# Attention with chunk selection and a gated FFN: 32-row score tiles for batch 0, plain v loads, later weight scaling, two jobs moved to ScalarE, finer preparation

## The chip, the cores and the metric

The kernel runs on one core of a Trainium2 chip. The metric is the device time of one execution in microseconds, the median of several runs. A run is called slow when it is over 1.5% above the fastest of its kernel; slow runs are left out of every comparison. The profile is one execution taken with the hardware profiler.

## The reference, cut to what matters

Four batches, eight heads, 768 positions, head size 64. Keys are grouped in 24 chunks of 32. For every query a bound on its score with each chunk is computed, the six best causal chunks are kept, and ordinary softmax attention runs over these. All heads of a token, side by side, then go through RMS normalisation and a gated FFN.

```python
ub = np.sum(np.maximum(q[:, :, :, None, :] * k_min[:, :, None, :, :],
                       q[:, :, :, None, :] * k_max[:, :, None, :, :]), axis=-1)
ub = np.where(causal, ub, -1000000000.0)
top_chunks = np.argsort(ub, axis=-1)[..., -top_k:]
scores = scale * np.matmul(q, k.transpose(0, 1, 3, 2))
scores = np.where(mask, scores, -1000000000.0)      # mask: chosen chunks, causal
# ... softmax, times v, heads side by side: x of 3072 x 512 ...
xn = x / np.sqrt(np.mean(x * x, axis=-1, keepdims=True) + 1e-06) * rms_g
g = xn @ w_gate
val = xn @ w_val
return (g * (1.0 / (1.0 + np.exp(-g))) * val) @ w_out
```

## The kernel before: the parts that matter

A *quad* is four heads of one batch, so there are eight quads, two per batch. The preparation of a quad loads K and Q, transposes them on VectorE in 32-row blocks (kT, qT), finds chunk minima and maxima, computes the bounds on TensorE (ubp), and ranks and chooses chunks on VectorE (mk, mt). The score matmuls want one head's 64 rows of K or Q plus 24 mask rows on partitions 0 to 87. The transposes leave two halves of 32 rows for four heads instead, so DMAs move them:

```python
def to_bf16(nm, dst, eng):
    def go():
        hb = half.tile([P, 2, S], BF16, name="hb")
        eng.tensor_copy(hb[:], st[nm + "T"][:])           # GpSimd
        for dh in range(2):
            for a in range(4):
                nc.sync.dma_start(out=dst[bi][32 * dh:32 * (dh + 1), a, :],
                                  in_=hb[32 * a:32 * (a + 1), dh, :])
    return go
# choose(): four more moves bring the chosen-chunk mask to QH[D:KR]
# scores(): per head and key block, one matmul of 88 rows
nc.tensor.matmul(sc[:, hl, 256 * e:256 * e + qn],
                 KH[bi][0:KR, a, kb * P:(kb + 1) * P], QH[bi][0:KR, a, qs:qs + qn],
                 start=True, stop=True)
```

v is loaded by casting DMAs from GpSimd's queue, ahead of the three FFN weights, which are casting DMAs too. The weights are multiplied by rms_g in place on VectorE (`fold_g`), directly after quad 0's preparation in the program. The tail of attention for one block of 128 tokens is:

```python
def rms(tt):
    nc.vector.tensor_tensor_reduce(out=junk[:], in0=xnat[tt][:], in1=xnat[tt][:],
        scale=1.0 / DM, scalar=0.0, op0=ALU.mult, op1=ALU.add, accum_out=ss_all[:, tt:tt + 1])
    # GpSimd: ri = (ss + eps) ** -0.5
    nc.vector.tensor_scalar(out=xs[:], in0=xnat[tt][:], scalar1=ri, scalar2=None, op0=ALU.mult)
    return xs
# turn(): TensorE transposes xs; after 512 tokens the FFN pieces gp, vp, ... op are queued
```

The emitted program is reordered: a scheduler places each instruction in its engine's queue by data dependencies and estimated times. The order on an engine is therefore not simply that of the text. In the traces below nothing passes an instruction that waits: while VectorE stood 13.25 us for wg, the choice of quad 0 stood behind it.

The softmax here doesn't subtract the row's maximum and nothing guards it: scores larger than these inputs give would overflow.

## Time and profile before

| | before |
|---|---|
| time, median of the runs beside the changed kernel's | 438.75 us |
| profiled span | 433.3 us |
| TensorE busy / VectorE / ScalarE / GpSimd | 320.6 / 258.9 / 178.7 / 183.4 us |
| first score matmul, first FFN matmul (gp) | 62.0 us, 107.4 us |

The first fence is the busy share of the span in 40 slices of 10.8 us, as tenths, of TensorE and of the core's DMA engines.

```profile
PE   0230084099897994888769986889899998789996
DMA  9999936170199254821562517102100020002002
```

In the first five slices the DMA engines are nearly full and TensorE nearly idle. The second fence is the table of engine time by stretch. Its columns are stretch, length, busy time with instruction counts for TensorE, its weight loads, VectorE, ScalarE and GpSimd, then clock, DMA share and GB/s. The cuts are the first score and the first gp.

```profile
0.00:62.00 62.00, 12.34 (x30) 7.66 (x30) 34.02 (x70) 1.28 (x1) 24.72 (x46) 0.75 1.14 162
62.00:107.40 45.40, 26.68 (x210) 19.00 (x211) 31.48 (x66) 19.47 (x24) 11.62 (x18) 0.62 0.45 101
107.40:433.30 325.90, 281.57 (x1905) 154.30 (x1903) 193.43 (x408) 157.90 (x240) 147.06 (x165) 0.94 0.30 60
```

For 107 us TensorE does 39 us of work. After that it is busy 281.6 of 325.9 us, idle 44.3. The timeline (start, duration, engine, line, instruction; in brackets the idle time before it and what ended it) shows what the start waits for:

```profile
32.99 2.21 DVE L392 TENSOR_SCALAR wg<-wg,rmsg 128x1536 bf16<-128x1536 bf16 x4 [13.25 <-DMA wg<-in_moe_w_gate_dram]
40.35 2.21 DVE L392 TENSOR_SCALAR wv<-wv,rmsg 128x1536 bf16<-128x1536 bf16 x4 [5.15 <-DMA wv<-in_moe_w_val_dram]
57.31 5.00 SPq L160 DMA_DIRECT2D QH_127<-hb  x8
62.04 0.33 PE L269 MATMUL sc<-QH_127,KH_124 88*128 88x256 bf16 x2 [0.52 <-DMA QH_127<-hb]
86.54 1.59 PE L269 MATMUL sc<-QH_128,KH_125 88*128 88x256 bf16 x6 [12.79 <-DMA QH_128<-hb]
```

VectorE stands 18.4 us for the weights, with quad 0's choice and quad 1's whole preparation behind it in its queue. The moves of a quad's Q then stand before its first scores. Later, TensorE's largest wait (engine, line, what it waited for: us in total, number, longest) and three groups of VectorE instructions (count, then busy us and mean ns of one, then idle time before) are these:

```profile
PE tp L342 <- DVE xs L331: 21.4, 12, 3.2
```

```profile
L323 DVE CUSTOM_DVE_ANT_0 junk<-xnat 128x512 bf16<-128x512 bf16 x24 | 22.6, 941 | 0.6
L280 DVE TENSOR_TENSOR pt<-pt,tri 128x1024 bf16<-128x1024 bf16 x24 | 19.1, 796 | 15.1 <-ACT pt L275 15.0
L380 DVE COPY osb<-op 128x512 f32<-128x512 f32 x24 | 16.6, 690 | 39.6 <-PE op L375 36.8 <-PE avn L298 2.8
```

### The profile page before, as it was taken

To read this page: it belongs to the slowest core of one execution; us is meant where nothing else is said; L and a number is where in the kernel's file an instruction comes from. 1 tells how busy PE (TensorE), PEld (TensorE's weight loads), DVE (VectorE), ACT (ScalarE), POOL (GpSimd) and SP (SyncE) were. 2 spreads that over 40 slices of the span, in tenths; PEclk is the share of its full clock that TensorE was granted. 3 is DMA by queue.
4 is the path that set the end of the run, shared out by engine and by line. 5 is a ranking of instruction groups with operands and counts; after the bars stand their busy time and mean duration, and the time that the engine had idled before them with its cause. 6 is when DMAs were issued, how large, how long until landed. Compare 5 with 4: busy or idle time off the path is not lost.

```text
span 433.3 us, 6106 instructions
## 1 busy us (share of the span) xinstructions
PE 320.6 (74%) x2144; PEld 181.0 (42%) x2144; DVE 258.9 (60%) x544; ACT 178.7 (41%) x265; POOL 183.4 (42%) x229
## 2 busy tenths in 40 slices
PE   0230084099897994888769986889899998789996
PEld 0120043067354463553435643554555554334442
DVE  5804947558858459759933798365746346623331
ACT  1000013075576322745831355532684456531750
POOL 9720210332597414563652168522443224530650
PEclk9985575558999896799959998799999999989999
DMA  9999936170199254821562517102100020002002
GB/s 163 181 210 210 109 101 137 48 173 20 31 145 120 51 166 78 97 73 28 130 59 84 147 40 73 39 0 78 67 2 8 29 75 1 2 0 98 0 2 97
DMA packets 52318, 34.32 MB, mean 79 GB/s; under 512 B 29504, under 2 KB 48192, under 8 KB 52288
## 3 DMA queue, kind: packets, MB, share of 16 engines
q1 hardware_dynamic: 24592, 26.07, 24.2%
q0 software_dynamic: 27696, 7.87, 19.2%
q8 instruction: 17, 0.28, 0.3%
q14 instruction: 13, 0.11, 0.1%
HBM read 28.31 MB, written 6.29 MB: 80 GB/s over the span
## 4 chain that ended last, share of the span: by engine, by line
PE 39%; DVE 27%; DMA 11%; issue 9%; POOL 8%; ACT 3%; SPq 3%; POOLq 0%; DVEq 0%; ACTq 0%
PE op L375 12%; PE gp L357 8%; PE vp L357 8%; DMA wv<-in_moe_w_val_dram 6%; DVE qT L148 4%; PE sc L269 4%; DVE tg L366 4%; PE ubp L209 4%; DVE xs L331 3%; PE avn L298 3%; DVE junk L323 3%; POOL ri_all L329 2%; DMA vext<-in_v_dram 2%; DVE kT L148 2%; DVE xnat L312 2%
## 5 line engine op out<-in xcount | busy, mean ns | idle before, releaser
L275 ACT ACTIVATE pt<-sc 128x768 bf16<-128x768 f32 (+1 forms) x96 | 84.3, 916 | 142.3 <-PE sc L269 140.6
L370 POOL TENSOR_TENSOR hh<-tg,vs 128x512 bf16<-128x512 bf16 x72 | 84.3, 1174 | 93.2 <-ACT vs L364 37.9
L357 PE MATMUL gp<-xsT,wg 128*128 128x512 bf16 x288 | 78.2, 392 | 3.7 <-DVE tg L366 2.1
L357 PE MATMUL vp<-xsT,wv 128*128 128x512 bf16 x288 | 76.7, 388 | 1.0 <-DVE tg L366 0.6
L366 DVE SCALAR_TENSOR_TENSOR tg<-th,gp 128x512 bf16<-128x512 bf16 x72 | 49.0, 681 | 46.3 <-ACT th L362 46.2
L375 PE MATMUL op<-wo,hh 128*128 128x512 bf16 x288 | 65.8, 383 | 0.0
L362 ACT ACTIVATE th<-gp 128x512 bf16<-128x512 f32 x72 | 43.3, 602 | 53.7 <-PE gp L357 53.6
L364 ACT ACTIVATE vs<-vp 128x512 bf16<-128x512 f32 x72 | 43.2, 600 | 21.4 <-PE vp L357 17.8
L298 PE MATMUL avn<-vext,pt 128*128 128x65 bf16 x672 | 38.6, 206 | 12.9 <-DVE xnat L312 6.2
L298 PEld LDWEIGHTS <-pt 128*128 128x128 bf16 x672 | 33.4, 106 | 28.9 <-DVE xnat L312 10.5
L357 PEld LDWEIGHTS <-wv 128*128 128x128 bf16 x288 | 28.8, 100 | 37.1 <-issue 6.0
L375 PEld LDWEIGHTS <-hh 128*128 128x128 bf16 x288 | 27.9, 99 | 31.9 <-issue 1.1
L380 DVE COPY osb<-op 128x512 f32<-128x512 f32 x24 | 16.6, 690 | 39.6 <-PE op L375 36.8
L357 PEld LDWEIGHTS <-wg 128*128 128x128 bf16 x288 | 27.1, 100 | 28.7 <-issue 7.5
L269 PE MATMUL sc<-QH_128,KH_125 88*128 88x256 bf16 (+1 forms) x144 | 22.4, 282 | 15.2 <-DMA QH_128<-hb 13.0
L209 PE MATMUL ubp<-qT,BD_131 128*128 128x288 f32 x32 | 11.1, 469 | 29.9 <-DVE qT L148 29.9
L269 PE MATMUL sc<-QH_127,KH_124 88*128 88x256 bf16 (+1 forms) x144 | 25.9, 319 | 3.8 <-DMA QH_127<-mt 2.5
L133 POOL DMA_DIRECT2D vext<-in_v_dram x32 | 27.5, 864 | 1.5 <-DMA vext<-in_v_dram 1.5
L280 DVE TENSOR_TENSOR pt<-pt,tri 128x1024 bf16<-128x1024 bf16 x24 | 19.1, 796 | 15.1 <-ACT pt L275 15.0
L342 PE MATMUL tp<-ident,xs 128*128 128x128 bf16 x96 | 11.4, 253 | 21.7 <-DVE xs L331 21.7
L148 DVE STREAM_TRANSPOSE qT<-qraw 128x768 f32<-128x768 f32 x16 | 23.8, 1532 | 4.6 <-POOL hb L157 4.0
L148 DVE STREAM_TRANSPOSE kT<-kraw 128x768 f32<-128x768 f32 x16 | 24.0, 1534 | 3.7 <-DMA kraw<-in_k_dram 3.7
(79 smaller groups left out, 347.6 us busy)
## 6 DMA issues: line engine op xcount, KB each, us to landing
kraw<-in_k_dram SPq DMA_DIRECT2D x32, 192.0 KB
qraw<-in_q_dram SPq DMA_DIRECT2D x32, 192.0 KB
out_dram<-osb SPq DMA_DIRECT2D x24, 256.0 KB
vext<-in_v_dram POOLq DMA_DIRECT2D x32, 96.0 KB, 6.0
wg<-in_moe_w_gate_dram POOLq DMA_DIRECT2D x1, 1536.0 KB, 21.2
wv<-in_moe_w_val_dram POOLq DMA_DIRECT2D x1, 1536.0 KB, 27.4
wo<-in_moe_w_out_dram POOLq DMA_DIRECT2D x1, 1536.0 KB, 32.0
KH_124<-hb SPq DMA_DIRECT2D x24, 48.0 KB
```

The costliest lines, as they stand in the source:

```text
L133: nc.gpsimd.dma_start(out=vext[:, :, a, 0:D], in_=v[b, 4 * g + a, :, :].rearrange("(blk pp) d -> pp blk d", pp=P),)
L148: nc.vector.transpose(out=st[nm + "T"][:, dh, :].rearrange("p (m r j) -> p m j r", r=32, j=4), in_=st[nm + "raw"][:, :, :, dh, :],)
L209: nc.tensor.matmul(ubp[:, 0:W], bd[:, t, :], rhs, start=(t == 0), stop=(t == 3))
L269: nc.tensor.matmul(sc[:, hl, 256 * e:256 * e + qn], KH[bi][0:KR, a, kb * P:(kb + 1) * P], QH[bi][0:KR, a, qs:qs + qn], start=True, stop=True,)
L275: nc.scalar.activation(out=pt[:, 2 * hp:2 * hp + 2, 0:W], in_=sc[:, :, 0:W], func=ACT.Exp, scale=SCALE,)
L298: nc.tensor.matmul(avn[:, a, :], pts[kg][:, a, off:off + P], vext[:, kb, a, :], start=(kb == 0 and a == 0), stop=(kb == nkb - 1 and a == 3 ...
L357: nc.tensor.matmul(ps[:], w[:, g, ht * P:(ht + 1) * P], x[:, g, :], start=(g == 0), stop=(g == NP - 1),)
L362: nc.scalar.activation(out=th[:], in_=gp[:], func=ACT.Tanh, scale=0.5)
L364: nc.scalar.activation(out=vs[:], in_=vp[:], func=ACT.Copy, scale=0.5)
L366: nc.vector.scalar_tensor_tensor(out=tg[:], in0=th[:], scalar=1.0, in1=gp[:], op0=ALU.add, op1=ALU.mult,)
L370: nc.gpsimd.tensor_tensor(out=hh[ht][:], in0=tg[:], in1=vs[:], op=ALU.mult)
L375: nc.tensor.matmul(op[:], hh[ht][:, t * P:(t + 1) * P], wo[:, ht, :], start=(ht == 0), stop=(ht == NHT - 1),)
```

## The change

The intent is to start attention earlier and to keep TensorE supplied. Batch 0 (quads 0 and 1) scores straight from the transposed layout on 32-row tiles, with the mask as a third 32-row product, so that no operand is moved. v comes by plain loads from SyncE's queue and is cast on GpSimd. The scaling by rms_g is emitted later. Square sums and output copies go to ScalarE. Preparation, score halves and rms transposes are spread over a unit. Cut to its core:

```diff
-    raw = ctx.enter_context(tc.tile_pool(name="raw", bufs=2))
+    raw = ctx.enter_context(tc.tile_pool(name="raw", bufs=5))        # now shared by k, q and v
-            nc.gpsimd.dma_start(
-                out=vext[:, :, a, 0:D],
+            nc.sync.dma_start(
+                out=t[:, :, a, :],
                 in_=v[...].rearrange("(blk pp) d -> pp blk d", pp=P),
+        def v_bf16():
+            nc.gpsimd.tensor_copy(VX[bi][:, :, :, 0:D], st["vraw"][:])
+                if tiled:                                            # to_bf16, quads 0 and 1
+                    nc.scalar.activation(out=dst[bi][:, 0:2, :], in_=st[nm + "T"][:], func=ACT.Copy)
+                    return
+            if tiled:                                                # choose
+                nc.vector.transpose(out=QH[bi][:, 2, Q0:S], in_=mk[:].rearrange("p j c -> p (j c)"))
+                return
+    def scores_tiled(u):                                             # per key block
+            for t in range(3):                                       # two halves of K.Q, then the mask
+                for a in range(4):                                   # head a on rows 32a to 32a+31
+                    r = slice(32 * a, 32 * (a + 1))
+                    o = sc[a // 2][:, a % 2, :]                      # a PSUM bank per head
+                    ...
-        if last:                                                     # causal product, four heads
+        if last:                                                     # now once per two heads
-        nc.vector.tensor_tensor_reduce(out=junk[:], ...)
+        nc.scalar.activation(out=junk[:], in_=xnat[tt][:], func=ACT.Square, ...)
-            nc.vector.tensor_copy(osb[:], op[:])
+            nc.scalar.activation(out=osb[:], in_=op[:], func=ACT.Copy)
-    fold_g()                                                         # after quad 0's preparation
+        if i >= 5 and folds:                                         # at the end of units 5 and 6
+            folds.pop(0)()
-            scores(units[i + 1])
+            scores(units[i + 1], 0)
         fill(1)
-        for f in late:
-            f()
+        prep_step(rate // 2)
+            scores(units[i + 1], 1)
         ...
         fill(1)
+        prep_step(rate - rate // 2)
+        while late and late[0][0] <= i:                              # the rms transposes
+            late.pop(0)[1]()
```

Not shown: the mask rows of a K buffer are now rewritten in every quad from 2 on, four small copies and a memset on VectorE. There are also fewer buffers for the exp tiles (4 instead of 5) and for the FFN's tiles (2 instead of 3).

More of the change, by code (lines that the diff above doesn't have):

```diff
@@ L55 @@
     persist = ctx.enter_context(tc.tile_pool(name="persist", bufs=1))
-    raw = ctx.enter_context(tc.tile_pool(name="raw", bufs=2))
+    raw = ctx.enter_context(tc.tile_pool(name="raw", bufs=5))
     tpose = ctx.enter_context(tc.tile_pool(name="tpose", bufs=1))
     half = ctx.enter_context(tc.tile_pool(name="half", bufs=1))
-    vpool = ctx.enter_context(tc.tile_pool(name="vpool", bufs=3))
     sel = ctx.enter_context(tc.tile_pool(name="sel", bufs=2))
-    ptp = ctx.enter_context(tc.tile_pool(name="ptp", bufs=5))
+    ptp = ctx.enter_context(tc.tile_pool(name="ptp", bufs=4))
     xnp = ctx.enter_context(tc.tile_pool(name="xnp", bufs=8))
@@ L65 @@
     hhp = ctx.enter_context(tc.tile_pool(name="hhp", bufs=NHT + 4))
-    ffn = ctx.enter_context(tc.tile_pool(name="ffn", bufs=3))
+    ffn = ctx.enter_context(tc.tile_pool(name="ffn", bufs=2))
     psS = ctx.enter_context(tc.tile_pool(name="psS", bufs=2, space=bass.MemoryType.PSUM))
@@ L84 @@
         nc.gpsimd.memset(own[32 * a:32 * (a + 1), a, :], 1.0)
+    chunkrow = const.tile([P, S], BF16, name="chunkrow")
+    nc.gpsimd.memset(chunkrow[0:32, :], MASKED)
+    nc.gpsimd.affine_select(
+        out=chunkrow[0:32, :], in_=chunkrow[0:32, :], compare_op=ALU.is_ge, fill=0.0,
+        base=0, pattern=[[1, S]], channel_multiplier=-CH,
+    )
+    nc.gpsimd.affine_select(
+        out=chunkrow[0:32, :], in_=chunkrow[0:32, :], compare_op=ALU.is_ge, fill=0.0,
+        base=CH - 1, pattern=[[-1, S]], channel_multiplier=CH,
+    )
+    for a in range(1, 4):
+        nc.vector.tensor_copy(chunkrow[32 * a:32 * (a + 1), :], chunkrow[0:32, :])
     eps6 = const.tile([P, 1], FP32, name="eps6")
@@ L93 @@
     NKB = 3
+    NTILED = NG
+    VX = [persist.tile([P, NT, 4, D + 1], BF16, name=f"VX{i}") for i in range(NKB)]
     KH = [persist.tile([P, 4, S], BF16, name=f"KH{i}") for i in range(NKB)]
@@ L122, in load @@
         for nm, src in (("k", k), ("q", q)):
-            t = raw.tile([P, NT, 4, 2, CH], FP32, name=nm + "raw")
+            t = raw.tile([P, NT, 4, 2, CH], FP32, name=nm + "raw", tag="raw")
             for a in range(4):
@@ L129, in load, with load_v @@
             st[nm + "raw"] = t
-        vext = vpool.tile([P, NT, 4, D + 1], BF16, name="vext")
-        nc.gpsimd.memset(vext[:, :, :, D:D + 1], 1.0)
+    def load_v(qd):
+        st = quads[qd]
+        t = raw.tile([P, NT, 4, D], FP32, name="vraw", tag="raw")
         for a in range(4):
-            nc.gpsimd.dma_start(
-                out=vext[:, :, a, 0:D],
-                in_=v[b, 4 * g + a, :, :].rearrange("(blk pp) d -> pp blk d", pp=P),
+            nc.sync.dma_start(
+                out=t[:, :, a, :],
+                in_=v[st["b"], 4 * st["g"] + a, :, :].rearrange("(blk pp) d -> pp blk d", pp=P),
             )
-        st["vext"] = vext
+        st["vraw"] = t
     def prep_pieces(qd):
@@ L152, in transpose_half, with chunk_rows @@
             return go
+        tiled = qd < NTILED
+        def v_bf16():
+            nc.gpsimd.tensor_copy(VX[bi][:, :, :, 0:D], st["vraw"][:])
+        def chunk_rows():
+            for a in range(4):
+                nc.vector.tensor_copy(KH[bi][D:KR, a, :], chunkrow[D:KR, :])
+            nc.vector.memset(QH[bi][D:KR, :, 0:Q0], 0.0)
         def to_bf16(nm, dst, eng):
             def go():
+                if tiled:
+                    nc.scalar.activation(out=dst[bi][:, 0:2, :], in_=st[nm + "T"][:], func=ACT.Copy)
+                    return
                 hb = half.tile([P, 2, S], BF16, name="hb")
@@ L241, in choose @@
                 )
-        return [
+        return ([] if tiled else [chunk_rows]) + [
             transpose_half("k", 0), transpose_half("k", 1),
@@ L248, in prep_pieces, with score_spans, scores @@
             to_bf16("q", QH, nc.gpsimd),
-            upper(0), upper(1), rank(0), rank(1), choose,
+            upper(0), upper(1), rank(0), rank(1), choose, v_bf16,
         ]
     xnat = {}
-    def scores(u):
+    def score_spans(u):
+        qd, qt, kg = u["key"]
+        last = kg == qt
+        for e in range(2):
+            qs = qt * 256 + (128 if (last and e) else 0)
+            yield e, 2 * kg + e, qs, (qt + 1) * 256 - qs
+    def scores_tiled(u):
+        qd, qt, kg = u["key"]
+        kb_, qb_ = KH[qd % NKB], QH[qd % NKB]
+        sc = [psS.tile([P, 2, 512], FP32, name="sc", tag="sc") for _ in range(2)]
+        for e, kb, qs, qn in score_spans(u):
+            ks = slice(kb * P, (kb + 1) * P)
+            ms = max(qs, Q0)
+            for t in range(3):
+                for a in range(4):
+                    r = slice(32 * a, 32 * (a + 1))
+                    o = sc[a // 2][:, a % 2, :]
+                    if t < 2:
+                        nc.tensor.matmul(
+                            o[:, 256 * e:256 * e + qn], kb_[r, t, ks], qb_[r, t, qs:qs + qn],
+                            start=(t == 0), stop=False, skip_group_check=True,
+                        )
+                    else:
+                        nc.tensor.matmul(
+                            o[:, 256 * e + ms - qs:256 * e + qn], chunkrow[r, ks],
+                            qb_[r, 2, ms:qs + qn],
+                            start=False, stop=True, skip_group_check=True,
+                        )
+        return sc
+    def scores(u, hp):
         qd, qt, kg = u["key"]
@@ L259, in scores @@
         W = 384 if last else 512
-        pt = ptp.tile([P, 4, 512], BF16, name="pt")
-        for hp in range(2):
+        if hp == 0:
+            u["pt"] = ptp.tile([P, 4, 512], BF16, name="pt")
+            if qd < NTILED:
+                u["sc"] = scores_tiled(u)
+        pt = u["pt"]
+        if qd < NTILED:
+            sc = u["sc"][hp]
+        else:
             sc = psS.tile([P, 2, 512], FP32, name="sc", tag="sc")
@@ L264, in scores @@
                 a = 2 * hp + hl
-                for e in range(2):
-                    kb = 2 * kg + e
-                    qs = qt * 256 + (128 if (last and e) else 0)
-                    qn = (qt + 1) * 256 - qs
+                for e, kb, qs, qn in score_spans(u):
                     nc.tensor.matmul(
@@ L274, in scores @@
                     )
-            nc.scalar.activation(
-                out=pt[:, 2 * hp:2 * hp + 2, 0:W], in_=sc[:, :, 0:W], func=ACT.Exp, scale=SCALE,
-            )
+        hs = slice(2 * hp, 2 * hp + 2)
+        nc.scalar.activation(out=pt[:, hs, 0:W], in_=sc[:, :, 0:W], func=ACT.Exp, scale=SCALE)
         if last:
-            dg = pt[:].rearrange("p a (e w) -> p a e w", e=2)[:, :, :, 0:P]
+            dg = pt[:, hs, :].rearrange("p a (e w) -> p a e w", e=2)[:, :, :, 0:P]
             nc.vector.tensor_tensor(
                 out=dg, in0=dg,
-                in1=tri[:].unsqueeze(1).unsqueeze(1).to_broadcast([P, 4, 2, P]),
+                in1=tri[:].unsqueeze(1).unsqueeze(1).to_broadcast([P, 2, 2, P]),
                 op=ALU.mult,
             )
-        u["pt"] = pt
     def values(u, s, avn, kgs, pts):
         qd, qt, _ = u["key"]
-        vext = quads[qd]["vext"]
+        vext = VX[qd % NKB]
         nkb = 2 * qt + s + 1
@@ L321, in rms @@
     def rms(tt):
-        junk = ev.tile([P, DM], BF16, name="junk")
-        nc.vector.tensor_tensor_reduce(
-            out=junk[:], in0=xnat[tt][:], in1=xnat[tt][:], scale=1.0 / DM,
-            scalar=0.0, op0=ALU.mult, op1=ALU.add, accum_out=ss_all[:, tt:tt + 1],
+        junk = ev.tile([P, DM], BF16, name="junk", bufs=1)
+        nc.scalar.activation(
+            out=junk[:], in_=xnat[tt][:], func=ACT.Square, scale=DM ** -0.5,
+            accum_out=ss_all[:, tt:tt + 1],
         )
@@ L387, in queue_ffn, with fold_g @@
             ffn_queue.append(lambda t=t: project(t))
-    def fold_g():
-        for w in (wg, wv):
-            for g in range(NP):
-                nc.vector.tensor_scalar(
-                    out=w[:, g, :], in0=w[:, g, :], scalar1=rmsg[:, g:g + 1],
-                    scalar2=None, op0=ALU.mult,
-                )
+    def fold_g(w):
+        for g in range(NP):
+            nc.vector.tensor_scalar(
+                out=w[:, g, :], in0=w[:, g, :], scalar1=rmsg[:, g:g + 1],
+                scalar2=None, op0=ALU.mult,
+            )
     load(0)
-    nc.sync.dma_start(out=rmsg[:], in_=moe_rms_g.rearrange("(g p) -> p g", p=P))
+    load(1)
     nc.vector.memset(BD[0][:], 0.0)
     nc.vector.memset(BD[1][:], 0.0)
-    nc.gpsimd.memset(KH[0][D:KR, 0, :], MASKED)
-    nc.gpsimd.affine_select(
-        out=KH[0][D:KR, 0, :], in_=KH[0][D:KR, 0, :], compare_op=ALU.is_ge, fill=0.0,
-        base=0, pattern=[[1, S]], channel_multiplier=-CH,
-    )
-    nc.gpsimd.affine_select(
-        out=KH[0][D:KR, 0, :], in_=KH[0][D:KR, 0, :], compare_op=ALU.is_ge, fill=0.0,
-        base=CH - 1, pattern=[[-1, S]], channel_multiplier=CH,
-    )
-    for i in range(NKB):
-        nc.vector.memset(QH[i][D:KR, :, 0:Q0], 0.0)
-        for a in range(4):
-            if i or a:
-                nc.vector.tensor_copy(KH[i][D:KR, a, :], KH[0][D:KR, 0, :])
-    load(1)
+    for i in range(NKB):
+        nc.vector.memset(VX[i][:, :, :, D:D + 1], 1.0)
+    for piece in prep_pieces(0)[:-1]:
+        piece()
+    load_v(0)
+    nc.sync.dma_start(out=rmsg[:], in_=moe_rms_g.rearrange("(g p) -> p g", p=P))
     nc.gpsimd.dma_start(out=wg[:], in_=moe_w_gate.rearrange("(kt p) n -> p kt n", p=P))
@@ L419 @@
     nc.gpsimd.dma_start(out=wo[:], in_=moe_w_out.rearrange("(kt p) n -> p kt n", p=P))
-    for piece in prep_pieces(0):
-        piece()
-    fold_g()
+    load_v(1)
+    prep_pieces(0)[-1]()
     NQD = B * NG
@@ L441 @@
     pts: dict = {}
-    scores(units[0])
+    scores(units[0], 0)
+    scores(units[0], 1)
+    folds = [lambda: fold_g(wg), lambda: fold_g(wv)]
     for i, u in enumerate(units):
@@ L450 @@
                 load(loaded)
+                load_v(loaded)
         if i + 1 < len(units):
             nxt = units[i + 1]["key"][0]
-            if nxt >= prep_next - 1:
-                if nxt == prep_next - 1:
-                    prep_step(len(prep_queue))
-            scores(units[i + 1])
+            if nxt == prep_next - 1:
+                prep_step(len(prep_queue))
+        ahead = first_of.get(prep_next - 1, i) - 2 - i
+        rate = -(-len(prep_queue) // max(1, ahead))
+        if i + 1 < len(units):
+            scores(units[i + 1], 0)
         fill(1)
-        for f in late:
-            f()
-        late = []
+        prep_step(rate // 2)
+        if i + 1 < len(units):
+            scores(units[i + 1], 1)
         if kg == 0:
@@ L466 @@
         values(u, 0, avn, [kg], pts)
-        rate = -(-len(prep_queue) // max(1, first_of.get(qd + 1, i + 1) - 1 - i)) if prep_queue else 0
-        rate = max(rate, 3)
-        prep_step(rate)
+        done = []
+        if kg == qt:
+            done.append(normalise(u, 0, avn))
         fill(1)
+        prep_step(rate - rate // 2)
+        while late and late[0][0] <= i:
+            late.pop(0)[1]()
         if kg == qt:
-            done = [normalise(u, 0, avn)]
             avn = psV.tile([P, 4, D + 1], FP32, name="avn", tag="av")
@@ L478 @@
                     xs = rms(tt)
-                    late.append(lambda tt=tt, xs=xs: turn(tt, xs))
-    for f in late:
+                    late.append((i + 1, lambda tt=tt, xs=xs: turn(tt, xs)))
+        if i >= 5 and folds:
+            folds.pop(0)()
+    for _, f in late:
+        fill(1)
         f()
```

## The prediction

> **What bounds the kernel now** (timeline and table of engine time by stretch; profiled span 433.3 us, timed median 437.6, so some 4 us lie outside the span).
>
> 1. Until the first FFN matmul (gp) at 107.4 us TensorE is mostly empty: 12.3 us busy in 0:62, 26.3 us in 62:107. The bound is a chain through VectorE and DMA. VectorE meets the folding of rms_g early in its in-order queue and stands 13.25 us for wg and 5.15 us for wv, until 40.3 us, with DMA over 90% busy. Only at 42.5 us does it go on to quad 0's selection and quad 1's preparation. The first score runs at 62.0 us, after eight QH moves. TensorE then waits 12.8 us, until 86.5, for quad 1's QH moves.
> 2. From 107 us on TensorE is the bound, with holes: idle about 44 of 326 us by the stretches. The largest wait is transposes for xs (21.4 us, 12 waits), the end of the chain square sum, GpSimd rsqrt, xs.
>
> **What the change does, costed.**
> - Folding moves behind both selections of batch 0: 18.4 us of waiting leave the start. On the path, all of it.
> - Batch 0 takes K, Q and mask straight from the transposes. Its 32 K/Q moves and 8 mask moves go; four ScalarE casts come (estimate 1.3 us each, from exp: 0.81 us for 768 columns, 0.97 for 1024). A unit has 24 score matmuls instead of 8 (which took 0.82 us). The Trainium skill ("TensorEngine Tiling (Array Packing)", Key Properties) says that row tiles run in parallel and that a mode switch drains the array. The four heads write four PSUM banks, so I expect 0.7 to 1.2 us a unit: neutral. No trace shows it yet.
> - v: 27.5 us of GpSimd issue go, eight casts of about 1.5 us come; off the path.
> - 24 square sums and 24 output copies (0.69 us each, 33 us) leave VectorE; about 29 us (0.6 each) come to ScalarE, 41% busy before. VectorE gains some 8 us of mask rows. The rms transposes come half a step later, preparation in smaller pieces. This should close 10 to 20 us of the holes; I take 16.
>
> **Sum.** In the instruction order that the changed kernel builds to: quad 0 selected near 28 us, first exp near 29, quad 1 selected near 48, first gp near 72 (estimate: 23 us of VectorE work lie between that selection and the first tg), 35 us earlier. Some 7 us more TensorE work is then left. Span 433 - 35 + 7 - 16 = 389, with the 4 us outside 393 us. Range 376 to 410. Chances: faster by over 2% 0.97, within 2% 0.02, slower 0.01.
>
> **What would show each step.**
> - No 13 and 5 us of VectorE idle before folding; folding near 45 to 57 us.
> - First score before 32 us, first gp at 65 to 80 us, no 12.8 us hole.
> - Transposes' wait on xs under 12 us; TensorE idle after the first gp 25 to 35 us.
> - Four row-tiled matmuls starting within about one matmul's time.
> - Busy: VectorE about 235 us, ScalarE 212, GpSimd 165.
>
> **What would make it wrong.** Row tiles running one after the other (estimate 2.5 us a unit, up to 20 us). q, k, v landing late behind weights that now start earlier. ScalarE holding exp behind a square sum. The five shared raw buffers holding loads back. The gain could shrink to 25 us; if the holes close fully it could reach 65.

## The result

| | before | after |
|---|---|---|
| time, median | 438.75 us | 394.05 us (393.0 to 396.0, four runs) |
| profiled span | 433.3 us | 391.3 us |
| TensorE / VectorE / ScalarE / GpSimd busy | 320.6 / 258.9 / 178.7 / 183.4 | 319.8 / 238.9 / 211.2 / 158.0 us |
| first score, first gp | 62.0, 107.4 us | 24.3, 71.8 us |

The ratio is 0.897, with a 95% interval of 0.890 to 0.905. Ratios here are the mean time of one kernel's fast runs over the mean of the other's fast runs of the same rounds, so not quite the ratio of the medians. The same views of the kernel after follow, slices first (9.8 us each):

```profile
PE   0165687998799649967798899798999999799996
DMA  8999999100068159111960196023110110002002
```

From the third slice on TensorE is busy for half a slice or more, while the loads still run. The table by stretch, cut at the first scores that need quad 0's choice and at the first gp:

```profile
0.00:27.40 27.40, 6.66 (x25) 4.22 (x26) 20.39 (x47) 4.25 (x3) 9.89 (x25) 1.00 1.02 213
27.40:71.80 44.40, 31.05 (x334) 19.88 (x334) 33.23 (x74) 21.71 (x31) 11.46 (x18) 0.59 1.05 198
71.80:391.30 319.50, 282.11 (x1981) 156.27 (x1978) 185.29 (x399) 185.28 (x308) 136.60 (x150) 0.95 0.28 66
```

The start is 35.6 us shorter (107.4 less 71.8), the rest 6.4 us (325.9 less 319.5). TensorE's work in the rest is the same (282.1 against 281.6 us). Its idle time there fell from 44.3 to 37.4 us. In the timeline the weights are folded without a wait, and no move stands before a score:

```profile
24.29 0.40 PE L306 MATMUL sc<-QH_134,KH_131 32*128 32x256 bf16 x8
27.40 0.21 PE L311 MATMUL sc<-QH_134,chunkrow 32*128 32x64 bf16 x4 [2.71 <-DVE QH_134 L266]
47.43 1.28 DVE L455 TENSOR_SCALAR wg<-wg,rmsg 128x1536 bf16<-128x1536 bf16 x1
71.84 1.75 PE L421 MATMUL gp<-xsT,wg 128*128 128x512 bf16 x4
```

TensorE's waits after the first gp, the counterpart of the wait on xs. The transposes' wait on xs is gone from the list of that window, and smaller waits have taken its place:

```profile
PE avn L362 <- DVE pt L345: 5.0, 7, 1.6
PE sc L335 <- DMA QH_134<-hb: 5.0, 2, 4.8
PE vp L421 <- DVE tg L430: 4.0, 4, 2.3
PE tp L406 <- DVE tg L430: 3.5, 5, 1.4
PE gp L421 <- DVE tg L430: 3.5, 4, 1.4
PE vp L421 <- ACT vs L428: 3.1, 4, 2.2
```

Of the three VectorE groups two have left for ScalarE. The third, the causal product, is cut in halves and costs more than before:

```profile
L387 ACT ACTIVATE junk<-xnat 128x512 bf16<-128x512 bf16 x24 | 15.2, 631 | 12.5 <-DVE xnat L376 12.5
L345 DVE TENSOR_TENSOR pt<-pt,tri 128x512 bf16<-128x512 bf16 x48 | 30.3, 637 | 21.1 <-ACT pt L342 20.7
L444 ACT ACTIVATE osb<-op 128x512 f32<-128x512 f32 x24 | 14.2, 600 | 34.4 <-PE op L439 31.1 <-issue 3.2
```

One thing the prediction had not seen in any trace can now be read: the cost of row tiles at full clock. This is a whole unit between values and gp. From its first start to the start of gp its 24 matmuls take 0.76 us (86.53 to 87.29). The last two lines are from the kernel before: a full unit of 8 matmuls of 88 rows took 0.88 us by the same measure (132.44 to 133.32).

```profile
86.53 0.40 PE L306 MATMUL sc<-QH_135,KH_132 32*128 32x256 bf16 x8
86.76 0.28 PE L311 MATMUL sc<-QH_135,chunkrow 32*128 32x256 bf16 x4
86.86 0.39 PE L306 MATMUL sc<-QH_135,KH_132 32*128 32x256 bf16 x8
87.08 0.28 PE L311 MATMUL sc<-QH_135,chunkrow 32*128 32x256 bf16 x4
87.29 0.39 PE L421 MATMUL gp<-xsT,wg 128*128 128x512 bf16 x1
132.44 1.04 PE L269 MATMUL sc<-QH_129,KH_126 88*128 88x256 bf16 x8
133.32 0.60 PE L357 MATMUL gp<-xsT,wg 128*128 128x512 bf16 x2
```

The prediction's 0.82 us for 8 matmuls is another thing: the units of before with that figure lie on the diagonal, so that half of their matmuls have 128 columns, and the figure runs to the modelled end of the last one. From start to start such a unit took 0.66 us. At 0.11 us for each of the 8, 24 matmuls one after the other would take about 2.6 us, an estimate. The four heads' tiles therefore ran side by side. This agrees with the Trainium skill, "TensorEngine Tiling (Array Packing)", Key Properties, which says that tiles operate independently. The change to row tiles at the start of the unit costs about 0.1 us more (see "Row tiles for all eight quads"). With it a full unit takes about 0.86 us, so the tiles are neutral.

### The profile page after: what moved, and what is told of

The parts are those of the page before. It is cut to its first block, busy times and chain, and to the rows that moved or that the text cites. A ratio compares the mean times of both kernels' runs of the same rounds, so it can differ in the third digit from the quotient of the medians.

```text
span 391.3 us, 6508 instructions
## 1 busy us (share of the span) xinstructions
PE 319.8 (82%) x2336; PEld 180.4 (46%) x2336; DVE 238.9 (61%) x518; ACT 211.2 (54%) x341; POOL 158.0 (40%) x193
## 4 chain that ended last, share of the span: by engine, by line
PE 44%; DVE 21%; DMA 11%; issue 7%; ACT 6%; SPq 5%; POOL 4%; POOLq 0%; DVEq 0%; ACTq 0%
PE op L439 15%; PE gp L421 8%; PE vp L421 8%; DMA kraw<-in_k_dram 8%; PE ubp L238 5%; PE sc L335 4%; DVE kT L164 3%; SPq L189 3%; DVE tg L430 3%; PE avn L362 3%; ACT pt L342 2%; DVE xs L395 2%; DMA vraw<-in_v_dram 2%; DVE pt L345 2%; POOL hh L434 2%
## 5 line engine op out<-in xcount | busy, mean ns | idle before, releaser
L342 ACT ACTIVATE pt<-sc 128x768 bf16<-128x768 f32 (+1 forms) x96 | 85.7, 918 | 67.6 <-PE sc L335 41.8
L421 PE MATMUL gp<-xsT,wg 128*128 128x512 bf16 x288 | 77.0, 388 | 6.3 <-DVE tg L430 3.5
L439 PE MATMUL op<-wo,hh 128*128 128x512 bf16 x288 | 67.3, 382 | 1.7 <-DVE tg L430 1.7
L345 DVE TENSOR_TENSOR pt<-pt,tri 128x512 bf16<-128x512 bf16 x48 | 30.3, 637 | 21.1 <-ACT pt L342 20.7
L439 PEld LDWEIGHTS <-hh 128*128 128x128 bf16 x288 | 27.5, 99 | 31.1 <-issue 2.4
L444 ACT ACTIVATE osb<-op 128x512 f32<-128x512 f32 x24 | 14.2, 600 | 34.4 <-PE op L439 31.1
L395 DVE TENSOR_SCALAR xs<-xnat,ri_all 128x512 bf16<-128x512 bf16 x24 | 13.8, 575 | 21.9 <-POOL ri_all L393 21.6
L207 POOL TENSOR_TENSOR dk<-kmx,kmn 128x48 f32<-128x48 f32 x8 | 2.6, 326 | 56.6 <-DVE kmn L198 40.9
L164 DVE STREAM_TRANSPOSE qT<-qraw 128x768 f32<-128x768 f32 x16 | 23.8, 1544 | 1.7 <-POOL hb L186 1.6
L387 ACT ACTIVATE junk<-xnat 128x512 bf16<-128x512 bf16 x24 | 15.2, 631 | 12.5 <-DVE xnat L376 12.5
L335 PE MATMUL sc<-QH_134,KH_131 88*128 88x256 bf16 x96 | 16.8, 301 | 5.3 <-DMA QH_134<-hb 5.0
L375 DVE RECIPROCAL rden<-avn 128x4 f32<-128x4 f32 x48 | 8.4, 175 | 21.0 <-PE avn L362 20.7
## 6 DMA issues: line engine op xcount, KB each, us to landing
wg<-in_moe_w_gate_dram POOLq DMA_DIRECT2D x1, 1536.0 KB, 14.3
```

Source lines behind the costliest of these rows:

```text
L164: nc.vector.transpose(out=st[nm + "T"][:, dh, :].rearrange("p (m r j) -> p m j r", r=32, j=4), in_=st[nm + "raw"][:, :, :, dh, :],)
L335: nc.tensor.matmul(sc[:, hl, 256 * e:256 * e + qn], KH[bi][0:KR, a, kb * P:(kb + 1) * P], QH[bi][0:KR, a, qs:qs + qn], start=True, stop=True,)
L342: nc.scalar.activation(out=pt[:, hs, 0:W], in_=sc[:, :, 0:W], func=ACT.Exp, scale=SCALE)
L345: nc.vector.tensor_tensor(out=dg, in0=dg, in1=tri[:].unsqueeze(1).unsqueeze(1).to_broadcast([P, 2, 2, P]), op=ALU.mult,)
L421: nc.tensor.matmul(ps[:], w[:, g, ht * P:(ht + 1) * P], x[:, g, :], start=(g == 0), stop=(g == NP - 1),)
L439: nc.tensor.matmul(op[:], hh[ht][:, t * P:(t + 1) * P], wo[:, ht, :], start=(ht == 0), stop=(ht == NHT - 1),)
```

## The experiments

The question was which parts of the change carry the 44.7 us. My theory was the sum of the prediction: the folding wait, then the moves, then the holes. The rivals were that one of these was hidden behind another, or that parts called "off the path" mattered. All runs below are medians of four. They were made on three chips. Most are set against the 394.05 us of after, measured earlier, so differences of 2 to 3 us between them are not firm. The ratio to before is a second measure. It was 0.897 for after, and undoing one part gave 0.898 (folding), 0.918 (tiles), 0.943 (v), 0.918 (sums and copies), 0.926 (whole pace) and 0.918 (early transposes).

### The folding alone, done on the kernel before

```diff
+    rmsgL = const.tile([P, NP], FP32, name="rmsgL")
+        nc.vector.tensor_copy(rmsgL[0:1, 0:1], quads[1]["mt"][0:1, 0:1])   # forces the order
+        nc.vector.tensor_copy(rmsgL[:], rmsg[:])                           # fold_g reads rmsgL
-    fold_g()
+        if i == 2:
+            fold_g()
```

Emitting `fold_g` later in the text was not enough: in a build (not run) that only did this, the scheduler still put the folding of wg ahead of quad 1's transposes. Hence the dependency.

> The kernel before with one part of the change alone: the folding of rms_g is forced behind quad 1's selection by a data dependency (a copy of rmsg that first takes one element of quad 1's mask). Theory (VectorE standing 18.4 us for the weights is the largest piece of the start): the 13 and 5 us waits go, first score before 45 us instead of 62, first gp near 85 us instead of 107, time near 417 us. Rival (the operand moves bound the start, the folding wait only hid them): first gp above 97 us, time above 428 us.

It took 420.65 us, 17.9 us less than before. The first score came at 44.2 us and the first gp at 92.4. The theory was right to about 4 us in the time. The first gp came 15 us earlier, less than I expected (near 85). Quad 1's moves still make a hole before its scores, 14.3 us against 12.8 in before; this explains at most 1.5 of the 7 us, and no run explains the rest. The profile is of the slowest of the four runs (424.83 us).

```profile
69.97 1.65 PE L270 MATMUL sc<-QH,KH 88*128 88x256 bf16 x6 [14.33 <-DMA QH<-hb]
```

### The folding put back to its old place, in the kernel after

The folding is emitted before quad 0's preparation, and two elements of the folded weights are copied into quad 0's bound tile before that is filled, so that the selection cannot pass it.

> The kernel after with the folding forced ahead of quad 0's selection on VectorE, where it stood before (a dependency through one element of ubn). Theory (the place cost much only because the weights landed at 33 and 40 us; here they are issued at 3 and 5 us and should have landed by 27 us): VectorE waits under 6 us for wv, time 396 to 401 us. Rival (the place itself is what costs, the weights land as late as before): VectorE waits 10 us or more, first gp above 84 us, time above 405 us.

```profile
36.66 2.21 DVE L458 TENSOR_SCALAR wg<-wg,rmsg 128x1536 bf16<-128x1536 bf16 x4 [0.94 <-DMA rmsg<-in_moe_rms_g_dram]
38.78 2.20 DVE L458 TENSOR_SCALAR wv<-wv,rmsg 128x1536 bf16<-128x1536 bf16 x4
```

It took 393.93 us, the same as after (my range was 396 to 401). VectorE did quad 1's K transposes, its chunk minima and maxima and half of its Q transposes first, then met weights that had already landed (at 17.9 and 26.8 us). Quad 0's choice came 19.5 us later than in after (46.9 against 27.4), the first gp 6 us later, at 77.9 us, and none of this showed in the median time. So the wait of before had two sufficient cures. One is the place of the folding (the run above). The other, it seems, is that the weights come earlier: after issues wg at 3.15 us and wv at 4.94 us, where before issued them at 11.79 and 12.91 us, behind v. This second cure is read from the trace; no run gave early weights to the kernel before.

### Batch 0 without the row tiles

```diff
-    NTILED = NG
+    NTILED = 0
```

> The kernel after with batch 0 scored as all other quads, on 88-row matmuls with K, Q and mask moved by DMA (NTILED = 0). Theory (the moves lie on the path of both quads of batch 0): first gp near 82 us instead of 72, time 401 to 406 us. Rival (once the folding is out of the way the moves hide behind VectorE's work): first gp under 75 us, time under 397 us.

```profile
76.23 0.95 PE L335 MATMUL sc<-QH,KH 88*128 88x256 bf16 x4 [15.91 <-DMA QH<-hb]
```

It took 402.85 us, 8.8 us more than after, inside the range expected. The mechanism shows as a hole of 15.9 us before quad 1's scores. The first gp came at 95.9 us (I had expected 82), 24 us later than in after, while the time rose only 8.8 us. The first gp is thus a poor measure by itself. What was done before it differs too: after its first gp this kernel had 304.7 us left, the kernel after 319.5.

### v by casting DMAs again

The plain loads and the GpSimd casts become casting DMAs from GpSimd's queue into the v tiles. The first version was wrong: it kept three v tiles, and the load of quad 3 overwrote quad 0's v before the last values of quad 0 were emitted. It gave a relative error of 0.36 and 411.23 us.

> The kernel after with v loaded by casting DMAs from the GpSimd queue straight into the bf16 tiles, as before; no plain load and no GpSimd cast. Theory (v is off the path): within 1% of after, 390 to 398 us, GpSimd busy up by about 16 us. Rival (the plain loads matter, by GpSimd's time and the start's DMA order): 400 us or more, with k, q or v of quad 1 landing later.

The repaired one has four v tiles and is correct. It also has four raw buffers instead of five, since v no longer uses them; the faulty version had five and took about as long.

```diff
-            nc.sync.dma_start(
-                out=t[:, :, a, :],
+            nc.gpsimd.dma_start(
+                out=VX[qd % 4][:, :, a, 0:D],
```

> The repaired a_v_cast_dma (that one overwrote quad 0's v with quad 3's while it was still read: wrong result, and a false wait): four v tiles instead of three, v by casting DMAs from the GpSimd queue as before, everything else as in after. Theory (the 411 us of the faulty kernel came mostly from that false wait; v's path itself is worth little): 394 to 400 us. Rival (the casting v DMAs go out ahead of the weights, delay them to 33 us or later and stop GpSimd behind DMA): 404 us or more.

It took 413.3 us, 19.3 us more than after. The theory fell; the rival holds. GpSimd's timeline shows how, and the last line is TensorE's:

```profile
8.44 0.76 POOL L469 DMA_DIRECT2D wg<-in_moe_w_gate_dram  x1
32.48 0.82 POOL L148 DMA_DIRECT2D VX<-in_v_dram  x1 [6.07 <-DMA wg<-in_moe_w_gate_dram]
41.71 0.82 POOL L148 DMA_DIRECT2D VX<-in_v_dram  x1 [8.40 <-DMA wv<-in_moe_w_val_dram]
52.28 4.19 POOL L148 DMA_DIRECT2D VX<-in_v_dram  x5 [9.75 <-DMA wo<-in_moe_w_out_dram]
57.38 4.21 PE L236 MATMUL ubp<-qT,BD 128*128 128x288 f32 x8 [19.99 <-POOL BD L208]
```

GpSimd issues five v loads behind the three weights, then stands until wg, wv and wo have landed, one after the other. Quad 1's bound matrix BD, also made by GpSimd, stands behind those loads in its in-order queue, and TensorE waits 20.0 us for it. In addition the weights go out behind quad 0's v and take longer: 23.8 us from issue to landing for wg, 14.3 us in after. So in this order the plain v loads are not a side matter: nothing on GpSimd's queue then stands behind the weights. The scheduler placed these loads itself, after the weights for quad 1; in the kernel before they went first. The 19 us are therefore the price of casting v loads in the new order, not the gain of plain loads over the old one.

### Square sums and output copies back on VectorE

```diff
-        nc.scalar.activation(out=junk[:], in_=xnat[tt][:], func=ACT.Square, ...)
+        nc.vector.tensor_tensor_reduce(out=junk[:], in0=xnat[tt][:], in1=xnat[tt][:], ...)
-            nc.scalar.activation(out=osb[:], in_=op[:], func=ACT.Copy)
+            nc.vector.tensor_copy(osb[:], op[:])
```

> The kernel after with the 24 square sums and 24 output copies back on VectorE. Theory (they lie on TensorE's path through xs): VectorE busy about 275 us, TensorE's wait for xs back over 10 us, time 399 to 405 us. Rival (neither engine is the bound, the place of the transposes in the program is what closed the holes): time within 3 us of after, wait for xs under 4 us.

It took 401.73 us, 7.7 us more than after, with VectorE busy 276.4 us. The size is as the theory said, but its path is not. TensorE's wait for xs came to 2.5 us only, while transposes waiting for a buffer that tg had to release went from 3.5 to 7.1 us. A busier VectorE delays tg, not mainly xs.

### The old pace, whole and in part

First the whole loop body of before: both score halves together, the old preparation rate, the transposes at the start of the next unit.

> The kernel after with the loop body of before: both score halves together, preparation at the old rate, the rms transposes at the start of the next unit; fold, tiles, v and ScalarE work as in after. Theory (the new pace closed the holes): TensorE's wait for xs back over 10 us, time 400 to 408 us. Rival (the engine split closed them): within 3 us of after, wait for xs under 4 us.

Then only the place of the transposes:

```diff
         fill(1)
+        while late and late[0][0] <= i:
+            late.pop(0)[1]()
         prep_step(rate // 2)
         ...
-        while late and late[0][0] <= i:
-            late.pop(0)[1]()
```

> The kernel after with one part of its pace undone: the rms transposes again come right after the first FFN piece of the next unit, not after its second half. Preparation is dealt out as in after. Theory (half a step more between square sum and transposes is what took TensorE's wait for xs from 21.4 to 0.4 us): wait for xs back over 8 us, time 398 to 404 us, so most of the 12 us that the whole old pace cost. Rival (the smaller pieces of preparation, not the place of the transposes, carry the gain): within 3 us of after.

The old pace took 405.76 us (11.7 more than after), the early transposes 400.42 us (6.4 more). Both gave a wrong result, with the same relative error of 0.059. Read from the program (not tested), the cause is this: with the transposes early, the first FFN piece is emitted in unit 6 before the folding of wv at that unit's end, and so uses unscaled columns. One of 72 FFN pieces reads weights a little early, so I use the times. TensorE's wait for xs is back in both runs, 14.8 us and here:

```profile
PE tp L406 <- DVE xs L395: 16.0, 12, 3.9
```

So the place of the transposes took that wait away. It is worth 6.4 of 11.7 us by the medians, and about 9 of 13 us by the ratios to before, so between half and three quarters of the pace. The rest is left for the smaller preparation pieces and split scores, which no run tested alone. The time rose less than the wait for xs did (about 16 us), because other waits shrank: TensorE's idle time rose only 2.3 us. Its busy time rose 6.1 us, at a mean granted clock of 0.906 against 0.916 in after.

### One causal product instead of two

```diff
-            dg = pt[:, hs, :].rearrange("p a (e w) -> p a e w", e=2)[:, :, :, 0:P]
+            dg = pt[:].rearrange("p a (e w) -> p a e w", e=2)[:, :, :, 0:P]     # after the second half
```

> The kernel after with one causal mask product for the four heads of a diagonal unit (128x1024) instead of two of 128x512, as before. Theory (splitting it doubled the times that VectorE, with two SBUF inputs, stands behind a GpSimd instruction: the mean went from 796 ns for 1024 columns to 637 ns for 512): VectorE busy falls 8 to 12 us, time 391 to 394 us. Rival (the halves let values start earlier, and that is worth more): 395 us or more.

```profile
L345 DVE TENSOR_TENSOR pt<-pt,tri 128x1024 bf16<-128x1024 bf16 x24 | 21.3, 888 | 12.1 <-ACT pt L342 12.0
```

It took 391.36 us (390.44 to 392.25), 2.7 us less than after, correct, with VectorE busy 230.6 us. This is the best version measured: its ratio to before is 0.893. The intervals of the two ratios overlap, so the gain over after is likely but small. Why halving costs more shows in after's timeline:

```profile
144.09 1.46 POOL L186 CAST hb<-kT 128x1536 bf16<-128x1536 f32 x1 [2.02 <-DMA QH_134<-hb]
144.20 1.62 DVE L345 TENSOR_TENSOR pt<-pt,tri 128x512 bf16<-128x512 bf16 x1 [3.37 <-ACT pt L342]
146.37 0.43 DVE L345 TENSOR_TENSOR pt<-pt,tri 128x512 bf16<-128x512 bf16 x1
```

The first product starts while a GpSimd cast runs and ends 0.27 us after it (145.82 against 145.55). The second, undisturbed, takes 0.43 us. The Trainium skill, "SBUF — State Buffer", section "SBUF: two separate sides", says that a VectorE instruction with two SBUF inputs and a GpSimd instruction that reads SBUF exclude each other for the whole instruction. This pair agrees with that, and so do the others. Of the 48 products of after, 28 started with no GpSimd computation under way and took 0.38 to 0.43 us. The other 20 started during one, and 19 of these ended 0.28 to 0.31 us after it. In the whole-mask version only 8 of 24 met one. The group rose from 19.1 to 30.3 us, and fell to 21.3 us here.

### Row tiles for all eight quads

`NTILED = B * NG`, with GpSimd casting K and Q of quads 2 to 7 straight into place, on the version above.

> The whole-mask version with all eight quads on 32-row score tiles, GpSimd casting K and Q of quads 2 to 7 straight into place: no K, Q or mask moves, no rewriting of mask rows. Theory (a unit costs TensorE the same either way, 0.76 against 0.82 us, so only the moves go, with their wait of 4 us and some 12 us of VectorE copies): 384 to 389 us against 391.4. Rival (between full-array FFN matmuls the row tiles cost a drain at each change, some 250 changes more): 392 us or more, TensorE busy up by over 6 us.

It took 407.95 us, 16.6 us more than the whole-mask version, and TensorE was busy 328.7 us against 320.8. My theory fell. The rival's numbers were met, but its mechanism carries only a small part. A change between row tiles and the full array can be read from the starts below: four tiles follow four tiles after 0.11 us (125.13 to 125.24), and the full-array matmul follows the last four after 0.21 us (125.46 to 125.67). On the way in, the first tile starts 0.31 us after the last full-array matmul, where such matmuls follow each other in 0.22 us. So a change costs about 0.1 us.

```profile
124.90 0.40 PE L309 MATMUL sc<-QH,KH 32*128 32x256 bf16 x8
125.13 0.28 PE L314 MATMUL sc<-QH,chunkrow 32*128 32x256 bf16 x4
125.24 0.39 PE L309 MATMUL sc<-QH,KH 32*128 32x256 bf16 x8
125.46 0.28 PE L314 MATMUL sc<-QH,chunkrow 32*128 32x256 bf16 x4
125.67 0.60 PE L442 MATMUL op<-wo,hh 128*128 128x512 bf16 x2
```

The trace has 130 changes, 98 more than the whole-mask version and not 250. That is some 10 us, an estimate; but the 36 units that are newly tiled save up to 0.2 us each in their matmuls, some 7 us, an estimate too. By these, about 3 of the 16.6 us are due to the changes. The mean granted clock was also lower, 0.881 against 0.916.

The largest new wait is that of vp for ScalarE's vs (3.1 us in after):

```profile
PE vp L424 <- ACT vs L431: 16.1, 12, 2.4
```

A tiled unit fills both score buffers at once, so its two exps come to ScalarE together and the next unit must wait for both. That fits this wait, but no run separates it from the changed order of loads, and the cause of most of the 16.6 us stays open.

### Extra matmuls to raise the clock

From 57 to 72 us after runs at a granted clock of 0.50, with TensorE busy 12.2 of 15 us. Eight unused matmuls of 384 columns were added to each of the first eight units of the whole-mask version.

> The whole-mask version with 8 extra matmuls of 384 columns on each of the first 8 units' exp tiles, results unused, to keep TensorE busy in the start. Theory (granted clock near 0.5 at 57 to 72 us is due to too little work before, and TensorE was 0.9 busy there): clock over 0.9 from 45 us on, first gp 3 to 5 us earlier, time 386 to 389 us. Rival (the extra work stands in the way of more than it gains, or the clock stays): 391 us or more.

The fence is that stretch of this run:

```profile
57.00:72.00 15.00, 10.21 (x146) 6.32 (x145) 10.48 (x15) 9.00 (x16) 5.66 (x11) 0.89 0.83 159
```

The clock rose to 0.89, from 0.50 in the whole-mask version. But the first gp came at 72.2 us, 1.1 us later than in that version. The one fast run took 392.3 us; the other three, 398.5 to 399.7 us, are counted slow. No gain is shown. In this run TensorE's clock was not what bounds the start, and the chain through VectorE, ScalarE and GpSimd fits what is left.

### A try at a better version

The whole-mask version, with mask rows written for quads 2 to 4 only and the four mask moves of a quad issued from ScalarE's queue.

> The whole-mask version with two more changes: the mask rows are written for quads 2 to 4 only (the buffers keep them for 5 to 7), and the four mask moves of a quad go out from ScalarE's queue, so that the eight QH moves need not stand behind them on SyncE's queue. Theory (the 4 us hole at the first score of quad 3 is serial issue, 12 moves of 0.6 to 0.8 us each on one queue after the mask is ready): that wait falls to about 1 us, time 386 to 389 us. Rival (ScalarE, now issuing 24 moves of some 0.7 us in order, holds up exp and tanh): 391 us or more.

It took 392.37 us (391.49 to 393.13), no better than the whole mask alone. VectorE fell to 224.8 us busy, but the hole before quad 3 grew to 7.4 us, from 4.1. The cause is a new wait. Between two K moves of quad 3 SyncE stood 10.9 us, until a mask move on ScalarE's queue had landed. The instruction records of the trace show that the program gave both moves the same DMA semaphore. GpSimd's cast of Q, which reuses the buffer of the K moves, then started only at 137.09 us, and the eight Q moves at 138.92, against 135.83 in the whole-mask version. So the shorter wait that the theory expected did not come. But the run tests neither the cost of serial issue nor the worth of the mask rows, because the edit brought a wait of its own.

## Why the prediction was right, and where its steps were not

The time, 393 us, was right to about 1 us (394.05). That it was so close is luck, as the errors below show; the range of 376 to 410 us is the fair measure. Several steps held. Quad 0 was chosen near 28 us (27.4), quad 1 near 48 (47.5), and the first gp came near 72 (71.8). The tiles were neutral for TensorE (about 0.86 us a full unit, 0.88 before). ScalarE was busy 211 us against 212 predicted, VectorE 239 against 235, GpSimd 158 against 165. The 12.8 us hole and the waits before folding are gone.

- **"Folding moves behind both selections ... On the path, all of it."** Right for the kernel before: alone it gained 17.9 us, of 18.4 us of waiting. Incomplete for the kernel after, where a fold forced ahead of quad 0's choice costs nothing, with weights that land earlier. The prediction listed earlier weights only as a risk. They look like a second cure of the same wait.
- **"v: 27.5 us of GpSimd issue go ...; off the path."** This step failed for the changed kernel: with casting v loads it takes 19.3 us more, through GpSimd's queue and TensorE's wait of 20.0 us for BD. The busy time did go; the worth was in what no longer stands behind a DMA. What plain loads alone would give the kernel before was not measured.
- **"This should close 10 to 20 us of the holes; I take 16."** Mis-sized: 6.9 us (44.3 to 37.4), outside the 25 to 35 us of idle that I named. The wait on xs did fall, below the 12 us I gave, but other waits came: tg, vs and the Q moves of quad 3.
- **"Some 7 us more TensorE work is then left."** Wrong: 0.5 us (282.1 against 281.6). With the last point I had -9 us for everything after the first gp, and it measured -6.4. Two errors partly cancelled.
- **"With the 4 us outside 393 us."** Wrong: about 1.7 us lie outside the span. I had set the median of other runs against the span of a profiled one. The 2.3 us cancelled the 2.3 us by which the span came out above 389.
- **Not seen at all:** cutting the causal product in halves cost VectorE 11 us of busy time, and some 2.7 us of run time.

The parts need not add up to the whole. Undone singly in the kernel after, the tiles cost 8.8 us, ScalarE's jobs 7.7, the pace 11.7, v 19.3 and the place of the folding nothing: 47.5 us, near the gain of 44.7 us. This nearness proves nothing: the folding alone was worth 17.9 us in the kernel before and nothing here, and the 19.3 us of v belong to the new order. Each figure holds with the other parts in place.

## What to carry to other kernels

A wait in a queue became a wait of what stood behind it: 18.4 us for VectorE's preparation in before, 20.0 us for BD behind casting v loads. When an instruction or a DMA issue is moved off an engine, ask what stood behind it there, not how long it was busy. When it is moved to another queue, ask what it shares there: a mask move on ScalarE's queue held SyncE for 10.9 us through a common semaphore. Where a wait has two sufficient cures, undoing one of them in the new kernel shows nothing, so also try that part alone on the old kernel. The date of the first matmul of a stage is a weak measure: here 24 us on that date were worth 9 us, and 6 us on it nothing that the median shows.

## What the Trainium skill lacked or had wrong

- "TensorEngine Tiling (Array Packing)", Key Properties, says that a change of tiling mode drains TensorE and gives no size. Here each change cost about 0.1 us, read from the starts of matmuls: 0.21 us instead of 0.11 us from the last four tiles to the next full-array matmul. The idle times of the profile do not show it, since it models the ends of matmuls.
- "TensorE: Matmul & The Clock Gate", "What's actually happening", says that about 3.4 us of sustained work release the throttle. Here TensorE showed 12.2 of 15 us busy (57 to 72 us) at a granted clock of 0.50 all through, and 10.2 of 15 us at 0.89 with the extra matmuls. Busy time at half clock is itself stretched: the first four gp matmuls, at the end of that stretch, took 1.75 us, and 1.02 us with the extra matmuls. The section gives no busy share that counts as sustained, so the busy share of a profile doesn't foretell the clock.
- I found on no page how many DMA semaphores a build gives to one engine. GpSimd stood 6.1, 8.4 and 9.8 us at its v loads, each time until the DMA issued eight before had landed. The instruction records show eight semaphores used in turn, each load waiting for the one that it will use itself. So here the number is the program's; what the queue could hold, no run tells.
- "SBUF — State Buffer", "SBUF: two separate sides", was borne out: a two-input product of 0.43 us took 1.62 us beside a 1.46 us GpSimd cast.
